# Turning the first groups' a and b with all 128 lanes, and one walk of 320 columns in the first batch's token mixing

## The chip, the cores and the metric

The kernel runs on one core of a Trainium2 chip (trn2). The metric is the device time of one execution in microseconds (us): the median of three runs. Engines are named as the profile does: PE is TensorE (PEld its weight loads), DVE is VectorE, ACT is ScalarE, POOL is GpSimd, SP is SyncE, which issues DMAs here.

## The reference

Three stages, all in float32 at the interface, with 4 batches, 8 heads, 768 steps, heads of 40, so rows of 320:

```python
# attention-like recurrence, per batch and head; state is 40 x 40
for t in range(S):
    y[t] = r[t] @ state
    Sa = state @ a[t]
    state = state * w[t][:, None] - outer(Sa, b[t]) + outer(v[t], k[t])
# x: the y of all heads, (4, 768, 320)
# first MLP block: mixing over the 768 steps (768 -> 256 -> 768), then over channels (320 -> 1536 -> 320)
u = x + (relu(x.T @ w_tok1) @ w_tok2).T
x = u + relu(u @ w_ch1) @ w_ch2
# second MLP block: normalised rows (320 -> 1280 -> 320)
x = x + relu(norm(x) * g_ln @ w2_ch1) @ w2_ch2
```

## The kernel before

The recurrence is done in chunks of 32 steps: within a chunk the state is not carried step by step, but a triangular system for the chunk is solved, and only from chunk to chunk is the state handed on (the chain). The 48 chain steps (function with L1069 and L1070) each treat half a pair of chunks for several heads; eight of them belong to one group G, and there are six groups. What is done for a group before its chain steps:

- `stack` (L781 to L802) loads w, b, a, k, v, r in 128 lanes of 32 steps, multiplies in the decays, splits each into high and low f16 parts in **one** buffer, o16 (L643, 128 lanes x 32 steps x 128), and stores it to scratch memory. The high parts are written by ACT (L795), the low part by DVE (L799) or POOL (L797). The next of the five can't be written before all readers of o16 are through.
- For groups 0 and 1, `turn` (L814 to L831) brings a and b from lanes x features to features x lanes on TensorE: o16 is the loaded operand, the identity the moving one. For later groups DMA transposes do this from scratch (`gram_load`, L833 to L840). The turned a stays for the chain ("at", eight single tiles, NA = 8); the turned b of groups 0 and 1 is put into the space of a weight matrix that is not needed yet ("d2").
- `gram` (L842 to L864) multiplies them into the 32 x 32 triangles, stores them (l_d); `solve` (L866 to L892) loads the triangles of the group ("ug"), sets diagonal and upper part with two selections on POOL (L870, L872), runs 30 pairs of DVE products and additions (L878, L880), and stores the result (t_d), from which the chain's operands are loaded ("tu").

Beside this run the decoding of the weights into f16 parts (L1153 load, L1158 and following on DVE, ACT) and, per batch, once its six pairs of chunks are through, the token mixing: `token_load` brings six row tiles "xt" of 128 x 320, `token1` multiplies them with w_tok1 into 256 hidden rows (two blocks NJ of 128) in two walks z over 160 columns each, with three-term f16 splits (L1245 on ACT, L1246 on DVE) and a relu (L1264, L1265); `token2` multiplies with w_tok2 (L1258) and adds (L1260). Then follow `feat_split` and the channel MLPs (L1307, L1310, L1317). Batch 0 uses the banks "pa", the others another one.

The order of the instructions on each engine is not that of the code: a planner (`Graph`, `fix_order`, L256 to L549) lists all instructions, gives each a duration from a table (`cost`, L201 to L235), schedules them by due times in several trials, takes the shortest, and writes the order of each engine as dependences without semaphores.

Of the kernel before, what the change touches and what calls it, by code (L numbers as in the profile page):

```python
# [20 lines left out]
def p2(n):  # L21
    return float(2.0 ** n)
# [178 lines left out]
def cost(i, engine):  # L201
# [23 lines left out]
        return 625 if len(rows) > 1 or 64 in rows or turned else 450, size / piece * (9 + piece / 27) / k * (1.6 if turned else 1.05)  # L225
    if engine == "PE":
        t = (free(i.outs[0]) + 6) / 2.4
        return (max(16, t / 2) if mode(i) else max(25, t)), 0
    part = 90 if min(x.ap[0][1] for x in aps) < 64 else 0
    if engine == "Activation":  # L230
# [322 lines left out]
def tile_main(  # L553
# [125 lines left out]
    PG = TG  # L679
    HC = C // 2  # L680
    RPP = PG * H * C
    NA = 8
    scr = {}
    l_d, t_d = {}, {}
    for G in range(NG // TG):
# [123 lines left out]
    def t_steps(G):  # L809
# [2 lines left out]
        st_i = {}  # L812

        def turn(n):  # L814
            for i in range(4):
                st = st_i.setdefault(i, {})
                if n == "a":
                    st[n] = stk.tile([128, TU * 128], F16, name="at", bufs=NA)
                    st_t.setdefault(4 * G + i, {})["a"] = st[n]
                else:  # L820
                    st[n] = wt["d2"].rearrange("p m l c -> p (m l c)")[:, i * TU * 128:(i + 1) * TU * 128]
                ls = slice(32 * i, 32 * i + 32)
                for t0 in (0, 16):
                    pt = ps_b.tile([128, 512], F32, name="pb", tag="b")[0:120].rearrange("p (l t) -> p l t", t=16)
                    for t in range(16):
                        nc.tensor.matmul(pt[:, :, t], o16[ls, t0 + t, 0:120], ident[ls, ls], start=True, stop=True)  # L826
                    dst = st[n][0:120].rearrange("p (l t) -> p l t", t=HC)[:, :, t0:t0 + 16]
                    if t0:
                        V.tensor_copy(dst, pt)
                    else:  # L830
                        A.activation(out=dst, in_=pt, func=ACTF.Copy)  # L831

        def gram_load(i):  # L833
            r0 = i * TU * 128
            st = st_i[i] = {}
            st["a"] = stk.tile([128, TU * 128], F16, name="at", bufs=NA)
            st["b"] = pre.tile([128, TU * 128], F16, name="tt_b", tag="st", bufs=2)
            for n in "ab":
                nc.sync.dma_start_transpose(out=st[n], in_=scr[n, G][r0:r0 + TU * 128, :])
            st_t.setdefault(4 * G + i, {})["a"] = st["a"]  # L840
# [68 lines left out]
    x_t = {}  # L909
# [326 lines left out]
    def token1(bb, z):  # L1236
        if z == 0:
            h16[bb] = moe.tile([128, NJ, 2, DM], F16, name="h16", bufs=1)
        n0 = DM // 2
        cs = slice(z * n0, (z + 1) * n0)  # L1240
        ps = token_bank(bb)[:, 0:NJ * n0].rearrange("p (j x) -> p j x", j=NJ)
        acc = Acc()
        for i in range(NT):
            x, o = x_t[bb][i][:, cs], moe.tile([128, 2, n0], F16, name="x16", bufs=2)
            nc.scalar.activation(out=o[:, 0, :], in_=x, func=ACTF.Copy, scale=p2(E_X))  # L1245
            nc.vector.scalar_tensor_tensor(out=o[:, 1, :], in0=x, scalar=p2(E_X),  # L1246
                                           in1=o[:, 0, :], op0=ALU.mult, op1=ALU.subtract)
            for jt in range(NJ):
                for n, (l, m) in enumerate(T3):
                    acc.mm(ps[:, jt, :], wt["t1"][:, i, l, jt * 128:(jt + 1) * 128], o[:, m, :], stop=i == NT - 1 and n == 2)  # L1250
        relu_split(ps, h16[bb][:, :, 0, cs], h16[bb][:, :, 1, cs])

    def token2(bb, i):
        x = x_t[bb][i]
# [22 lines left out]
    def feat_split(srcs, e, first=None):  # L1277
        ut = moe.tile([128, 6, TB * 128], F16, name="ut", bufs=2)
        for i, s in enumerate(srcs):
            u16 = moe.tile([128, 2, 384], F16, name="u16", bufs=2)  # L1280
            if first is not None:
                square("u", first + i, u16[:, 0, 0:64], s[:, 0:320:5])
            if first is None:
# [203 lines left out]
```

## Time and profile before

| | |
|---|---|
| median of three runs | 1177.3 us (1176.42 to 1181.52) |
| the profiled execution | 1180.47 us, span 1178.8 us, mean granted TensorE clock 0.979 |
| busy time in the span | PE 904.6, PEld 734.4, DVE 770.8, ACT 507.4, POOL 206.3 us |
| DMA | 161.67 MB in 356903 packets, 66.6% of the 16 engines' span on the hardware queue |

Busy time is summed over the whole span; its share hides that the stages have different limits, so the stages are shown apart in the rows below. A matmul's duration in a row runs from start to result; matmuls overlap, so that a group's duration divided by its count is the pace.

### The profile page before, as it was taken

To read this page: it belongs to the slowest core of one execution; us is meant where nothing else is said; L and a number is where in the kernel's file an instruction comes from. 1 tells how busy PE (TensorE), PEld (TensorE's weight loads), DVE (VectorE), ACT (ScalarE), POOL (GpSimd) and SP (SyncE) were. 2 spreads that over 40 slices of the span, in tenths; PEclk is the share of its full clock that TensorE was granted. 3 is DMA by queue.
4 is the path that set the end of the run, shared out by engine and by line. 5 is a ranking of instruction groups with operands and counts; after the bars stand their busy time and mean duration, and the time that the engine had idled before them with its cause. 6 is when DMAs were issued, how large, how long until landed. Compare 5 with 4: busy or idle time off the path is not lost.

```text
span 1178.8 us, 39814 instructions
## 1 busy us (share of the span) xinstructions
PE 904.6 (77%) x17422; PEld 734.4 (62%) x17422; DVE 770.8 (65%) x1936; ACT 507.4 (43%) x1105; POOL 206.3 (17%) x212
## 2 busy tenths in 40 slices
PE   0631450155588878899899999898999999999996
PEld 0620440154577756677677777676777888787774
DVE  6679485868977695657865689656964563443432
ACT  1443333455655453554445545554553343332221
POOL 0235450332000631034120052201000000000000
PEclk9999999999999989989999999999999999999998
DMA  5569826879998778958999757897565532221111
GB/s 159 155 171 242 189 72 193 260 146 182 229 190 162 179 157 198 186 102 160 154 204 162 166 118 170 144 174 173 111 115 93 80 47 47 52 44 21 36 17 26
DMA packets 356903, 161.67 MB, mean 137 GB/s; under 512 B 327536, under 2 KB 336752, under 8 KB 353136
## 3 DMA queue, kind: packets, MB, share of 16 engines
q1 hardware_dynamic: 356720, 159.04, 66.6%
q8 instruction: 138, 2.26, 0.8%
q14 instruction: 45, 0.37, 0.1%
HBM read 71.70 MB, written 50.59 MB: 104 GB/s over the span
## 4 chain that ended last, share of the span: by engine, by line
PE 34%; DVE 8%; DMA 4%; ACT 2%; issue 1%; SPq 1%; POOL 0%; DVEq 0%; ACTq 0%
PE pb L1317 12%; PE pa L1307 9%; PE ch L935 4%; PE pa L1310 3%; PE ps L935 3%; DVE ug L880 1%; DVE hh L1265 1%; PE ps L1014 1%; PE ps L1258 1%; DMA xt<-x_d 1%; DVE tmp L878 1%; DVE u L890 1%; PE ps L993 1%; DMA x<-in_v_dram 1%; DMA x<-in_r_dram 1%
## 5 line engine op out<-in xcount | busy, mean ns | idle before, releaser
L1317 PE MATMUL pb<-c,hh 128*128 128x320 f16 x864 | 179.5, 305 | 2.8 <-ACT hh L1264 2.1
L1317 PEld LDWEIGHTS <-hh 128*128 128x128 f16 x1584 | 153.4, 99 | 39.1 <-ACT hh L1264 3.0
L1265 DVE SCALAR_TENSOR_TENSOR hh<-pa,hh 128x512 f16<-128x512 f32 x132 | 90.6, 687 | 125.8 <-ACT hh L1264 125.3
L1307 PE MATMUL pa<-ut,c 128*128 128x256 f16 x864 | 159.4, 275 | 4.8 <-issue 2.4
L1264 ACT ACTIVATE hh<-pa 128x512 f16<-128x512 f32 x132 | 78.5, 595 | 173.0 <-PE pa L1310 168.2
L1317 PE MATMUL pb<-d,hh 128*128 128x320 f16 x720 | 147.6, 301 | 0.9 <-ACT hh L1264 0.7
L1307 PE MATMUL pa<-ut,d 128*128 128x256 f16 x720 | 137.7, 279 | 9.1 <-DVE hh L1265 6.2
L1307 PEld LDWEIGHTS <-c 128*128 128x128 f16 x864 | 83.4, 99 | 25.7 <-issue 5.3
L1307 PEld LDWEIGHTS <-d 128*128 128x128 f16 x720 | 69.8, 100 | 25.8 <-issue 8.2
L795 ACT ACTIVATE o<-x 128x2560 f16<-128x2560 f32 x30 | 69.9, 2331 | 20.9 <-DMA x<-in_a_dram 7.2
L880 DVE TENSOR_TENSOR ug<-ug,tmp 128x30 f32<-128x30 f32 (+9 forms) x180 | 73.0, 405 | 1.4
L878 DVE TENSOR_TENSOR tmp<-ug 128x30 f32<-128x30 f32 (+9 forms) x180 | 69.5, 386 | 4.2 <-POOL ug L872 2.6
L1343 POOL TENSOR_TENSOR y<-ve,mhalf 128x2 f32<-128x2 f32 x12 | 8.9, 741 | 353.3 <-DVE stats L1339 214.6
L826 PE MATMUL pb<-ident,o 32*120 32x32 f16 x512 | 50.3, 283 | 23.8 <-POOL o L797 13.2
L1310 PE MATMUL pa<-ut,c1t 128*128 128x256 f16 x288 | 65.4, 276 | 0.0
L826 PEld LDWEIGHTS <-o 32*120 32x120 f16 x512 | 49.1, 214 | 24.7 <-POOL o L797 13.4
L797 POOL TENSOR_TENSOR o<-x,o 128x1280 f16<-128x1280 f32 x15 | 49.7, 3314 | 59.2 <-ACT o L795 40.3
L935 PEld LDWEIGHTS <-srx 64*64 64x64 f16 x2304 | 51.8, 122 | 10.8 <-issue 8.1
L1310 PE MATMUL pa<-ut,d1t 128*128 128x256 f16 x240 | 55.5, 277 | 0.0
L858 PE MATMUL pa<-at,d 120*32 120x32 f16 (+1 forms) x384 | 5.2, 206 | 63.9 <-DVE lc L862 61.3
L935 PE MATMUL ch<-vx,sak 64*64 64x40 f16 x1152 | 33.9, 198 | 26.4 <-DVE n L1087 16.7
L722 POOL TENSOR_TENSOR x<-x,sx 128x1280 f32<-128x1280 f32 x10 | 33.1, 3307 | 115.7 <-DMA x<-in_k_dram 63.5
(204 smaller groups left out, 1914.2 us busy)
## 6 DMA issues: line engine op xcount, KB each, us to landing
raw<-in_moe_w_ch_dram SPq DMA_DIRECT2D x30, 320.0 KB
scr_b<-o SPq DMA_DIRECT2D x6, 1024.0 KB
scr_k<-o SPq DMA_DIRECT2D x6, 1024.0 KB
scr_v<-o SPq DMA_DIRECT2D x6, 1024.0 KB
scr_r<-o SPq DMA_DIRECT2D x6, 1024.0 KB
t_d<-u SPq DMA_DIRECT2D x24, 256.0 KB
tu<-t_d SPq DMA_DIRECT2D x24, 256.0 KB
scr_a<-o SPq DMA_DIRECT2D x4, 1024.0 KB
```

The costliest lines, as they stand in the source:

```text
L722: eng.tensor_tensor(out=o, in0=x, in1=y, op=ALU.mult)
L795: A.activation(out=hi2, in_=x.unsqueeze(2).broadcast_to([128, HC, 2, D]), func=ACTF.Copy, scale=p2(e))
L797: P.tensor_tensor(out=o16[:, :, lo:lo + D], in0=x, in1=o16[:, :, 0:D], op=ALU.subtract)
L826: nc.tensor.matmul(pt[:, :, t], o16[ls, t0 + t, 0:120], ident[ls, ls], start=True, stop=True)
L878: V.tensor_tensor(out=tv, in0=ug[:, 0:s, s:s + 1].broadcast_to([128, s, n]), in1=ug[:, s:s + 1, s + 1:32].broadcast_to([128, s, n]), op=AL ...
L880: V.tensor_tensor(out=ug[:, 0:s, s + 1:32], in0=ug[:, 0:s, s + 1:32], in1=tv, op=ALU.add)
L935: m = nc.tensor.matmul(out, lhsT, rhs, start=start, stop=stop, skip_group_check=True)
L1264: nc.scalar.activation(out=hi, in_=ps, func=ACTF.Relu)
L1265: nc.vector.scalar_tensor_tensor(out=lo, in0=ps, scalar=0.0, in1=hi, op0=ALU.max, op1=ALU.subtract)
L1307: nc.tensor.matmul(o, w1[:, f, l, ms], ut[:, f + 3 * q, :], start=n == 0, stop=False)
L1310: nc.tensor.matmul(o, w1t[:, ms], ut[:, 2 + 3 * q, :], start=False, stop=q == 1)
L1317: nc.tensor.matmul(pb[i][:, 0:DM], hh[:, l, c0:c0 + 128], w2[:, m0 + s, q, :], start=m0 + s == 0 and n == 0, stop=m0 + s == nm - 1 and n == 2)
```

## The change

Three edits in the kernel, and one in the planner's table. (1) `turn` for a group writes one tile of 4 x 1024 columns ("at", two buffers in all, which the DMA-transposed groups share), and each matmul takes all 128 lanes of o16 at once with the whole identity: 32 matmuls of 128 columns for a turn where there were 128 of 32 columns, with an output column in every fourth word of PSUM (every sixteenth before). Eight evictions of 120 x 512 as before, each now for four steps of all lanes. (2) the planner's table gives such a matmul with separated outputs at least 100. (3) `token1` for batch 0 walks the tiles once with 320 columns into two banks. The other batches are unchanged. (4) The splits of that walk share a tag with those of `feat_split`.

```diff
--- before.py
+++ after.py
@@ -225,6 +225,8 @@
         return 625 if len(rows) > 1 or 64 in rows or turned else 450, size / piece * (9 + piece / 27) / k * (1.6 if turned else 1.05)
     if engine == "PE":
         t = (free(i.outs[0]) + 6) / 2.4
+        if i.outs[0].ap[-1][0] > 1:
+            return max(100, t), 0
         return (max(16, t / 2) if mode(i) else max(25, t)), 0
     part = 90 if min(x.ap[0][1] for x in aps) < 64 else 0
     if engine == "Activation":
@@ -679,7 +681,7 @@
     PG = TG
     HC = C // 2
     RPP = PG * H * C
-    NA = 8
+    a_t = {}
     scr = {}
     l_d, t_d = {}, {}
     for G in range(NG // TG):
@@ -812,28 +814,30 @@
         st_i = {}
 
         def turn(n):
+            if n == "a":
+                o = a_t[G] = stk.tile([128, 4, TU * 128], F16, name="at", bufs=2)
+            else:
+                o = wt["d2"].rearrange("p m l c -> p (m l c)")[:, 0:4 * TU * 128].rearrange("p (i c) -> p i c", i=4)
             for i in range(4):
-                st = st_i.setdefault(i, {})
+                st_i.setdefault(i, {})[n] = o[:, i]
                 if n == "a":
-                    st[n] = stk.tile([128, TU * 128], F16, name="at", bufs=NA)
-                    st_t.setdefault(4 * G + i, {})["a"] = st[n]
+                    st_t.setdefault(4 * G + i, {})["a"] = o[:, i]
+            dst = o[0:120].rearrange("p i (l t) -> p (i l) t", t=HC)
+            for t0 in range(0, HC, 4):
+                pt = ps_b.tile([128, 512], F32, name="pb", tag="b")[0:120].rearrange("p (l t) -> p l t", t=4)
+                for t in range(4):
+                    nc.tensor.matmul(pt[:, :, t], o16[:, t0 + t, 0:120], ident, start=True, stop=True)
+                if t0 % 8:
+                    V.tensor_copy(dst[:, :, t0:t0 + 4], pt)
                 else:
-                    st[n] = wt["d2"].rearrange("p m l c -> p (m l c)")[:, i * TU * 128:(i + 1) * TU * 128]
-                ls = slice(32 * i, 32 * i + 32)
-                for t0 in (0, 16):
-                    pt = ps_b.tile([128, 512], F32, name="pb", tag="b")[0:120].rearrange("p (l t) -> p l t", t=16)
-                    for t in range(16):
-                        nc.tensor.matmul(pt[:, :, t], o16[ls, t0 + t, 0:120], ident[ls, ls], start=True, stop=True)
-                    dst = st[n][0:120].rearrange("p (l t) -> p l t", t=HC)[:, :, t0:t0 + 16]
-                    if t0:
-                        V.tensor_copy(dst, pt)
-                    else:
-                        A.activation(out=dst, in_=pt, func=ACTF.Copy)
+                    A.activation(out=dst[:, :, t0:t0 + 4], in_=pt, func=ACTF.Copy)
 
         def gram_load(i):
             r0 = i * TU * 128
             st = st_i[i] = {}
-            st["a"] = stk.tile([128, TU * 128], F16, name="at", bufs=NA)
+            if i == 0:
+                a_t[G] = stk.tile([128, 4, TU * 128], F16, name="at", bufs=2)
+            st["a"] = a_t[G][:, i]
             st["b"] = pre.tile([128, TU * 128], F16, name="tt_b", tag="st", bufs=2)
             for n in "ab":
                 nc.sync.dma_start_transpose(out=st[n], in_=scr[n, G][r0:r0 + TU * 128, :])
@@ -1236,6 +1240,10 @@
     def token1(bb, z):
         if z == 0:
             h16[bb] = moe.tile([128, NJ, 2, DM], F16, name="h16", bufs=1)
+        if bb == 0:
+            if z == 0:
+                wide(bb)
+            return
         n0 = DM // 2
         cs = slice(z * n0, (z + 1) * n0)
         ps = token_bank(bb)[:, 0:NJ * n0].rearrange("p (j x) -> p j x", j=NJ)
@@ -1250,6 +1258,20 @@
                     acc.mm(ps[:, jt, :], wt["t1"][:, i, l, jt * 128:(jt + 1) * 128], o[:, m, :], stop=i == NT - 1 and n == 2)
         relu_split(ps, h16[bb][:, :, 0, cs], h16[bb][:, :, 1, cs])
 
+    def wide(bb):
+        ps = [token_bank(bb) for _ in range(NJ)]
+        for i in range(NT):
+            x, o = x_t[bb][i], moe.tile([128, 2, DM], F16, name="x16", tag="u16", bufs=2)
+            nc.scalar.activation(out=o[:, 0, :], in_=x, func=ACTF.Copy, scale=p2(E_X))
+            nc.vector.scalar_tensor_tensor(out=o[:, 1, :], in0=x, scalar=p2(E_X),
+                                           in1=o[:, 0, :], op0=ALU.mult, op1=ALU.subtract)
+            for jt in range(NJ):
+                for n, (l, m) in enumerate(T3):
+                    nc.tensor.matmul(ps[jt][:, 0:DM], wt["t1"][:, i, l, jt * 128:(jt + 1) * 128], o[:, m, :],
+                                     start=i == 0 and n == 0, stop=i == NT - 1 and n == 2)
+        for jt in range(NJ):
+            relu_split(ps[jt][:, 0:DM], h16[bb][:, jt, 0], h16[bb][:, jt, 1])
+
     def token2(bb, i):
         x = x_t[bb][i]
         pu = token_bank(bb)
@@ -1277,7 +1299,7 @@
     def feat_split(srcs, e, first=None):
         ut = moe.tile([128, 6, TB * 128], F16, name="ut", bufs=2)
         for i, s in enumerate(srcs):
-            u16 = moe.tile([128, 2, 384], F16, name="u16", bufs=2)
+            u16 = moe.tile([128, 2, 384], F16, name="u16", tag="u16", bufs=2)
             if first is not None:
                 square("u", first + i, u16[:, 0, 0:64], s[:, 0:320:5])
             if first is None:
```

The planner moves other instructions as a result. On POOL, between the suffix and inverse work of group 1's decays (L722, L724 after; the two lines more in the code shift all later numbers), the order before had the two selections of group 0's solve ("ug") ahead of the low parts of b and a (o) of group 1:

```order
L722 TENSOR_TENSOR wf<-wf 128x7x40
L722 TENSOR_TENSOR x<-x,sx 128x1280
L722 TENSOR_TENSOR wf<-wf 128x40
L870 AFFINE_SELECT ug<-ug 128x1024
L722 TENSOR_TENSOR wf<-wf 128x40
L872 AFFINE_SELECT ug<-ug 128x1024
L797 TENSOR_TENSOR o_118<-x,o_118 128x32x40
L722 TENSOR_TENSOR wf<-wf 128x40 x5
L722 TENSOR_TENSOR wf<-wf 128x8x120
L722 TENSOR_TENSOR x<-x,wf 128x1280
L797 TENSOR_TENSOR o_118<-x,o_118 128x32x40
```

and the order after has the low parts of b (the first o) and of a (the second) ahead of the selections:

```order
L724 TENSOR_TENSOR wf<-wf 128x7x40
L799 TENSOR_TENSOR o_118<-x,o_118 128x32x40
L724 TENSOR_TENSOR wf<-wf 128x40 x7
L724 TENSOR_TENSOR wf<-wf 128x8x120
L724 TENSOR_TENSOR x<-x,wf 128x1280
L799 TENSOR_TENSOR o_118<-x,o_118 128x32x40
L874 AFFINE_SELECT ug<-ug 128x1024
L876 AFFINE_SELECT ug<-ug 128x1024
L724 TENSOR_TENSOR x<-x,sx 128x1280
L799 TENSOR_TENSOR o_118<-x,o_118 128x32x40
```

The two selections moved behind two writes of o16 and the work between them. On SP, the load of "ug" of group 0 stood ahead of the store of r of group 0 (scr_r_123) and the store of b of group 1 (scr_b_129):

```order
L868 DMA ug<-l_d_125 128x1024
L714 DMA scr_r_123<-o_118 128x4096
L711 DMA x<-in_a_dram 32x1x1280 x2
L954 DMA_TRANSPOSE kt<-scr_k_120 128x1024
L1153 DMA raw<-in_moe_w_ch_dram 64x768 x4
L1153 DMA raw<-in_moe_w_ch_dram 128x640
L954 DMA_TRANSPOSE rt<-scr_r_123 128x1024
L711 DMA x<-in_a_dram 32x1x1280 x2
L711 DMA x<-in_k_dram 32x1x1280
L714 DMA scr_b_129<-o_118 128x4096
```

and now stands behind both, and behind the fourth store of the triangles (l_d):

```order
L716 DMA scr_r_123<-o_118 128x4096
L713 DMA x<-in_a_dram 32x1x1280 x2
L1157 DMA raw<-in_moe_w_ch_dram 64x768 x4
L868 DMA l_d_125<-sab 128x8x32
L1157 DMA raw<-in_moe_w_ch_dram 128x640
L958 DMA_TRANSPOSE kt<-scr_k_120 128x1024
L958 DMA_TRANSPOSE rt<-scr_r_123 128x1024
L713 DMA x<-in_a_dram 32x1x1280 x2
L713 DMA x<-in_k_dram 32x1x1280
L716 DMA scr_b_129<-o_118 128x4096
L713 DMA x<-in_k_dram 32x1x1280
L872 DMA ug<-l_d_125 128x1024
```

The load moved behind both stores. On DVE, the token mixing of batch 0 before: L1246 are the low parts of the second walk's tiles, between the pairs of a solve and the chain, L1265 a walk's relu, L1260 the first addition of the second matrix:

```order
L1246 SCALAR_TENSOR_TENSOR x_12691<-xt,x_12691 128x160
L880 TENSOR_TENSOR ug<-ug,tmp 128x12x19
L980 TENSOR_TENSOR srx<-ps,srx 128x512
L878 TENSOR_TENSOR tmp<-ug 128x234
L1265 SCALAR_TENSOR_TENSOR h_7189<-pa,h_7189 128x2x160
L880 TENSOR_TENSOR ug<-ug,tmp 128x13x18
L878 TENSOR_TENSOR tmp<-ug 128x238
L880 TENSOR_TENSOR ug<-ug,tmp 128x14x17
L878 TENSOR_TENSOR tmp<-ug 128x240
L880 TENSOR_TENSOR ug<-ug,tmp 128x15x16
L1260 SCALAR_TENSOR_TENSOR xt<-pa,xt 128x320
```

and after, where L1266 is the last tile's low part of the single walk, L1287 its two relus and L1282 the addition:

```order
L1266 SCALAR_TENSOR_TENSOR x_6844<-xt,x_6844 128x320
L1142 SCALAR_TENSOR_TENSOR yo<-ps,yw 128x320
L1074 SCALAR_TENSOR_TENSOR r_6593<-ch,r_6593 128x160
L882 TENSOR_TENSOR tmp<-ug 128x30
L884 TENSOR_TENSOR ug<-ug,tmp 128x30
L1287 SCALAR_TENSOR_TENSOR h_6796<-pa,h_6796 128x320 x2
L882 TENSOR_TENSOR tmp<-ug 128x58
L1080 SCALAR_TENSOR_TENSOR sas<-ch,sas 128x4x40
L884 TENSOR_TENSOR ug<-ug,tmp 128x2x29
L1282 SCALAR_TENSOR_TENSOR xt<-pa,xt 128x320
```

The additions stand ahead of the solve's pairs that were before them, and fewer rows lie between a relu and the first addition. The later walks of the other batches are as they were.

## Rows read from the trace of the kernel before

**Rows 1.** Stages: us, busy us (instructions) of PE, PEld, DVE, ACT, POOL; clock; DMA; GB/s.

```profile
0.00:121.00 121.00, 32.84 (x548) 31.19 (x548) 86.48 (x187) 42.54 (x76) 40.34 (x68) 1.00 0.73 181
121.00:199.00 78.00, 27.95 (x384) 27.16 (x385) 48.53 (x121) 25.23 (x40) 27.68 (x11) 1.00 0.51 140
199.00:246.00 47.00, 10.17 (x420) 9.06 (x420) 37.92 (x84) 26.63 (x55) 16.59 (x6) 1.00 0.78 222
246.00:427.00 181.00, 134.51 (x3539) 115.28 (x3539) 146.30 (x362) 96.92 (x227) 34.68 (x37) 1.00 0.97 188
427.00:1012.00 585.00, 545.30 (x11111) 427.62 (x11110) 388.30 (x1013) 276.64 (x625) 84.92 (x87) 0.96 0.73 135
1012.00:1178.00 166.00, 153.79 (x1422) 124.07 (x1421) 63.30 (x174) 39.38 (x85) 2.07 (x3) 0.98 0.17 31
```

**Rows 2.** Timeline, DVE: chain steps 2, 16 and 32 of 48.

```profile
245.74 0.30 DVE L1070 SCALAR_TENSOR_TENSOR r<-ch,r 128x160 f16<-128x160 f32 x1
...
427.08 0.32 DVE L1070 SCALAR_TENSOR_TENSOR r<-ch,r 128x160 f16<-128x160 f32 x1
...
730.66 0.33 DVE L1070 SCALAR_TENSOR_TENSOR r<-ch,r 128x160 f16<-128x160 f32 x1
```

**Rows 3.** Timeline, group 0: start us, us, instruction [idle before <-releaser].

```profile
48.13 2.34 ACT L795 ACTIVATE o<-x 128x2560 f16<-128x2560 f32 x1 [1.00 <-PE pb L826]
...
52.88 11.89 PE L826 MATMUL pb<-ident,o 32*120 32x32 f16 x128 [4.79 <-DVE o L799]
...
64.87 2.34 ACT L795 ACTIVATE o<-x 128x2560 f16<-128x2560 f32 x1 [1.06 <-PE pb L826]
```

**Rows 4.** A turn's evictions, tile pb (count: min/median/max ns, first to last).

```profile
L829 DVE CAST d<-pb x8: 691/692/692, 37.5 to 140.8; 120x512 f16<-120x512 f32 x8
```

**Rows 5.** Matmuls near the new one: tile pb, timeline, page's group (mean ns).

```profile
L1100 PE MATMUL pb<-ident,sas x48: 314/314/363, 233.0 to 376.9; 128*120 128x128 f16 x48
...
397.72 0.63 PE L1100 MATMUL ps<-ident,sas 128*120 128x128 f16 x4
...
L1317 PEld LDWEIGHTS <-hh 128*128 128x128 f16 x1584 | 153.4, 99 | 39.1 <-ACT hh L1264 3.0
```

**Rows 6.** Timeline, turns of group 1.

```profile
131.69 9.06 PE L826 MATMUL pb<-ident,o 32*120 32x32 f16 x96
...
150.08 6.23 PE L826 MATMUL pb<-ident,o 32*120 32x32 f16 x64 [9.33 <-POOL o L797]
```

**Rows 7.** Timeline, DVE: first product and last addition of the solve, a wait between.

```profile
120.99 0.19 DVE L878 TENSOR_TENSOR tmp<-ug 128x30 f32<-128x30 f32 x1 [2.63 <-POOL ug L872]
...
189.71 0.33 DVE L1158 TENSOR_SCALAR wst<-raw 128x320 int32<-128x320 int32 x1 [13.75 <-DMA raw<-in_moe_w_ch_dram]
...
198.27 0.20 DVE L880 TENSOR_TENSOR ug<-ug,tmp 128x30 f32<-128x30 f32 x1
```

**Rows 8.** Timeline, token mixing of batch 0 on ACT, PE and DVE.

```profile
409.89 0.42 ACT L1264 ACTIVATE h<-pa 128x320 f16<-128x320 f32 x1
421.19 0.44 ACT L1264 ACTIVATE h<-pa 128x320 f16<-128x320 f32 x1
...
418.12 1.76 PE L935 MATMUL pa<-x,t 128*128 128x160 f16 x12 [1.97 <-DVE x L1246]
...
424.92 0.49 DVE L1260 SCALAR_TENSOR_TENSOR xt<-pa,xt 128x320 f32<-128x320 f32 x1
...
425.62 1.68 PE L1258 MATMUL pa<-h,t 128*128 128x320 f16 x6
427.19 0.84 PE L1258 MATMUL pa<-h,t 128*128 128x320 f16 x5
...
440.21 1.06 PE L1307 MATMUL pa<-ut,c 128*128 128x256 f16 x6
```

**Rows 9.** Issues of SyncE for the tile at, and for the solves' tile ug.

```profile
L839 SPq DMA_TRANSPOSE at<-scr_a x16: 1173/1709/4062, 254.8 to 734.5; - x16
...
L868 SPq DMA_DIRECT2D ug<-l_d x6: 529/608/1790, 112.0 to 797.3; - x6
```

## Prediction

> **What bounds the kernel now.** I read first the table of stages [rows 1]. The reader is to see six stages with different limits. From 427 us on TensorE (PE) is busy 545.30 of 585.00 us and then 153.79 of 166.00: what remains there as idle time is 39.7 + 12.2 = 51.9 us, so after 427 the end is set by the amount of TensorE work. Before 427 it isn't: TensorE works 32.84 of 121, 27.95 of 78, 10.17 of 47 and 134.51 of 181 us. Time is to be had or lost there, and 427 us is where the channel MLPs, which can fill TensorE, begin (first matmul of L1307 at 440.21 [rows 8]). What holds the early stages is, in turn: the preparation of the first two groups, in which b, a, k, v, r pass one after the other through the one buffer o16 (0 to 121); the triangular solve of group 0 (121 to 199); the way from it to the chain (199 to 246: the second chain step is at 245.74 [rows 2]); and then DMA, busy 0.97, with VectorE (DVE) at 146.30 of 181.00 us (246 to 427).
>
> The chain's steps [rows 2] are the clock of the middle: DVE instructions of L1070, the second at 245.74, the sixteenth at 427.08. Then come the rows of the turns [rows 3 to 6], of the solve [rows 7], of the token mixing of batch 0 [rows 8] and of the loads of later groups [rows 9].
>
> **Edit 1, the turns of a and b of groups 0 and 1.** Before, one turn is 128 matmuls with 32 rows and 32 columns each. It takes 11.89 us where it runs alone [rows 3] (93 ns apiece); 64 of them take 6.23 and 96 take 9.06 [rows 6]. Meanwhile o16 can't be overwritten: the next scaling by ACT (L795) starts at 48.13 and at 64.87, and the profile names the turn as what released it [rows 3]. After, a turn has 32 matmuls with 128 columns, and eight evictions as before, of the same size. The nearest row to the new matmul is L1100: four matmuls with identity, 128x128, in 0.63 us [rows 5]; one of them lasts 0.314 at the longest usual [rows 5], so the pace is (0.63 − 0.31) / 3 = 0.107 us and 32 make 3.4 us. But two "pb" banks alternate, and each bank has to be evicted before its next filling: 4 × 0.107 + 0.2 to the last result + 0.69 for the VectorE eviction [rows 4] + about 0.3 of hand-over = 1.6 us for a bank, so eight fillings over two banks take 4 × 1.6 = 6.4 us. The 0.2 is 0.314 less the pace; the 0.3 is an estimate, two releases from engine to engine at 0.10 (the turn ends at 52.88 + 11.89 = 64.77, ACT starts at 64.87 [rows 3]) and as much again. I take 6.4, which gains 11.9 − 6.4 = 5.5 us a turn. Ends: a gain of 6.5 if the hand-over is free, and none at all if the output, written now every 16 bytes, is slow. No row shows a 128-column matmul into separated words; the row that bounds it is the old turn, whose outputs lie 64 bytes apart: 32 columns in 93 ns are at most 93 / 32 = 2.9 ns a column, or 0.37 us for 128 columns, 11.9 us a turn, the old time. I go by the low end of the price, since the old pace has another explanation in the same rows: each matmul also loads 120 weight columns, and the loads of L1317, 128 columns and no separated words, average 99 ns [rows 5].
>
> The Trainium skill, "PSUM — Partial Sum Buffer", section "Specifications (TRN2)", says that PSUM lines are 8 bytes long and that any non-contiguous pattern slows matmuls significantly. By it each column would pay, and the turn would stay near 11.9 us. "TensorE: Matmul & The Clock Gate", section "LDWEIGHTS", has a load take about its columns over 1.2 in ns, which is 100 ns for 120 columns, and leaves nothing of the old pace for the separated words; the 93 ns agree with it. No run here tells which holds for 128 columns; the first is the third rival below.
>
> The buffer's chain is b0, a0, ..., b1, a1. The turn of b0 gains about 1 (ACT waited 1.00 on PE there [rows 3]); a0 and b1 gain 5.5 each. So o16 of a1, ready when its turn starts at 150.08 [rows 6], is ready 12 us earlier, at 138; the turn of a1 gives 5.5 more to what follows.
>
> **Edit 2, the order around the solve.** With the turns shorter, GpSimd (POOL) gets the two selections of the solve of group 0 after the low part of a1 instead of before that of b1, and SyncE the load of the solve's tile ("ug") after the store of b1. Before, the solve's first DVE product is at 120.99, right after the second selection [rows 7]. After, the selections stand behind a1's write: 138 + 2.7 = 141, some 20 us later. The solve before ran from 120.99 to its last addition at 198.27 [rows 7], 77.3 us, in which VectorE was busy 48.53 of 78.00 [rows 1]: 29.5 us were idle time, 13.75 of them in one piece on a weight load that stands in DVE's queue ahead of the solve's rest [rows 7]. Started at 141 it ends at 141 + 48 = 189 if every wait is over by then, and at 218 if none is. I take the middle, 204: about 6 us late (bounds −9 and +20). Queued behind it are the t_d stores on SyncE and the first chain steps, so this shift is passed on to the step at 245.74.
>
> **Edit 3, what VectorE has to do between chain steps 2 and 16.** In the new order 321 DVE instructions stand between the second and the sixteenth L1070, where 362 stood. 41 × 146.30 / 362 = 41 × 0.404 = 16.6 us of work are gone from a stretch in which DVE is busy 0.81. Most of it is weight decoding (11 instead of 16 groups) and solving (34 pairs instead of 45) that now lie in the earlier trough, so it costs nothing there: DVE has 29.5 us idle in 121 to 199. But DMA is busy 0.97 of the same stretch and its bytes do not change. Late next, if DVE isn't, is DMA. I count half: −8 us (bounds 0 and −16.6).
>
> **Edit 4, token mixing of batch 0.** Before, the six row tiles are walked twice with 160 columns. The first walk's relu is at 409.89, the second's at 421.19 [rows 8], and the second mixing matrix follows. Now one walk with 320 columns ends where the first ended, plus a second relu: 36 matmuls with 320 columns instead of 72 with 160, about the same time on TensorE (12 of the old take 1.76 us, 0.15 each or 10.6 for 72; six 320-column matmuls take 1.68 in the same stretch [rows 8], 10.1 for 36), and six ACT and six DVE instructions less, worth 2 or 3 us beside other work. It starts the second matrix and with it the MLP at 440.21 about 10 us earlier against its tiles (bounds 0 and −11.3). The clock matters for the size: just there six matmuls of L1258 take 1.68 us and the next five 0.84 [rows 8], 0.28 and 0.17 apiece: times of the lower (1.2 GHz) and of the upper level (2.4), though the granted clock of the stage reads 1.00 throughout [rows 1]. What comes earlier runs part of the way at the lower level. The tiles of the walk share a two-deep ring with the feature splits; that is covered, as the splits come after the mixing.
>
> **Edit 5, one "at" tile with two buffers instead of eight singles.** A load for group G waits until all four pairs of group G−2 are through with theirs. Group 5 is the tightest: group 3 ends with chain step 32, at 730.66 [rows 2]; before, the last single was loaded at 734.5, and the load of its solve is issued at 797.3 [rows 9]. All four loads can follow 730.66 and their products still come before 797.3. I cost it at nothing; the cover is those 60 us.
>
> **Sum.** +6 (solve) − 8 (VectorE) − 10 (mixing) = −12 us at the point where TensorE fills. What comes earlier lands in a stage where TensorE was already busy 134.51 of 181.00 us, and 51.9 us of idle remain behind it that depend on other waits; I let about 0.8 pass: −10. The profiled execution took 1180.47 us (span 1178.8, 1.7 around it), 3.2 above the median of 1177.3. 1177.3 − 10 = **1167 us**.
>
> **Rivals.**
> First (the forecast, 0.50): as summed, own range 1156 to 1176.
>
> Second, nothing arrives (0.20): the solve keeps its waits and its 77 us (+20), and this uses up −8 and −10: 1177, between 1172 and 1182. For it: the waits inside the solve name DMA, which is no faster. Against: DMA's share is 0.51 in 121 to 199, so loads there can come earlier.
>
> Third, slower (0.15): the separated words make a new matmul take 0.37 us. Then the turn stays at 11.9, a1 is written at 150 and the solve, behind it in the new order, starts at 152.7, 31.7 late; with its 77 us and −8, −10 that is +13.7 at 427, × 0.8 = +11: 1188. It decides from where the turn takes more than the 6.4 us of the sum; at 8 us the loss is some +4. For it speaks that no row shows this output; against it the weight loads.
>
> Fourth, all gains pass (0.10): the solve ends at 189 (−9), DVE gives 16.6 and mixing 11.3: −37 × 0.8 = −30: 1148.
>
> Fifth (0.05): the two-deep ring of "at" stops SyncE's queue, in which loads for everything else stand, behind a pair's last use; a stop of one pair, two chain steps of (427.08 − 245.74) / 14 = 13 us [rows 2], against the 12 of the sum gives +14 × 0.8 = +11, 1188. Against it stand the 60 us above.
>
> **How the numbers follow.** A measurement of this kernel can't tell less than 0.5%, 5.9 us, from no change. Faster than 1171.4: four fifths of the first (0.40), all of the fourth (0.10), a little of the second (0.03): 0.53. Slower than 1183.2: 0.13 of the third, 0.04 of the fifth, 0.03 of the second: 0.20. The rest, 0.27, is no change. The range leaves out most of the fourth and half of the third: 1151 to 1187.
>
> **What would show it.** Right if a turn of group 0 takes 5 to 8 us, the second selection of the first solve ends at 138 to 145, the solve ends by 210, and the second chain step is at 240 to 256; if the sixteenth step is no later than 425; if the first second-matrix addition (L1260 before, at 424.92 [rows 8]) is at 408 to 418; and if TensorE's idle time from there to the end is still about 52 us. The step on edit 1 is wrong if the turns take 10 us or more; that on edit 2 if the solve ends after 215 or before 190; that on edit 3 if DMA takes up the room and the steps from 2 to 16 stay 181 us apart; the last factor if the MLP begins 10 us earlier and the end does not move.

## The result, and the profile after

The changed kernel takes 1158.0 us in the median (1155.46 to 1161.89, four runs) beside 1176.9 of the kernel before on the same chip: a ratio of 0.985, 95% interval 0.981 to 0.989. The forecast was 1167, its range 1151 to 1187. The profiled execution took 1157.96 us, its span 1156.3, where it was 1178.8. Line numbers from here on are those of the changed kernel, unless another run is named: `turn` is L829 (matmul), L831 and L833 (evictions), a chain step L1074, the mixing L1270 (first matrix), L1286 (relu), L1280 and L1282 (second matrix and its addition), the MLP begins with L1329.

The same stages as in [rows 1], the last one ending with the span (us; busy us and instructions of PE, PEld, DVE, ACT, POOL; granted clock; DMA share; GB/s):

```profile
0.00:121.00 121.00, 29.68 (x404) 24.95 (x404) 89.25 (x198) 48.84 (x85) 47.80 (x74) 0.68 0.82 207
121.00:199.00 78.00, 9.21 (x192) 8.37 (x193) 64.28 (x155) 31.36 (x54) 22.89 (x8) 0.52 0.63 177
199.00:246.00 47.00, 14.15 (x508) 12.37 (x509) 33.83 (x72) 24.90 (x52) 19.38 (x14) 0.50 0.80 203
246.00:427.00 181.00, 143.12 (x3695) 118.55 (x3692) 134.59 (x349) 96.69 (x226) 26.26 (x28) 0.59 0.92 173
427.00:1012.00 585.00, 544.88 (x11105) 434.93 (x11103) 384.82 (x1008) 273.35 (x614) 82.11 (x86) 0.95 0.71 133
1012.00:1156.00 144.00, 132.91 (x1111) 106.65 (x1108) 54.49 (x151) 32.09 (x70) 2.07 (x3) 0.98 0.15 28
```

The reader is to see the trough of 121 to 199: VectorE is busy 64.28 us instead of 48.53, DMA 0.63 instead of 0.51. That is work brought forward, and 427 to 1012 is as full as before (544.88 against 545.30); the time is missing at the end, 144 us instead of 166. The clock column is not to be compared in the early stages: it reads about 0.5 to 0.7 here and 1.00 before, yet the same matmul of L1104 (L1100 before) on "pb" has a median of 314 ns in both. The trace's clock records begin at 34.26 us here and only at 427.07 in the kernel before; ahead of its first record the column reads 1.00.

The chain and the mixing, from the timeline of DVE, ACT and PE (start, duration), for [rows 2, 8]:

```profile
238.68 0.32 DVE L1074 SCALAR_TENSOR_TENSOR r<-ch,r 128x160 f16<-128x160 f32 x1
...
406.81 0.31 DVE L1074 SCALAR_TENSOR_TENSOR r<-ch,r 128x160 f16<-128x160 f32 x1
...
392.97 0.44 ACT L1286 ACTIVATE h<-pa 128x320 f16<-128x320 f32 x1 [0.36 <-PE pa L1270]
...
395.87 0.49 DVE L1282 SCALAR_TENSOR_TENSOR xt<-pa,xt 128x320 f32<-128x320 f32 x1 [0.92 <-PE pa L1280]
...
413.51 1.49 PE L1329 MATMUL pa<-ut,c 128*128 128x256 f16 x6
```

Step 2 is 7.1 us earlier than before, step 16 20.3, the first addition of the second matrix 29.1 (it was at 424.92), the MLP 26.7, the end of the span 22.5.

The four turns and what stands behind them, from the timeline of the same kernel, for [rows 3, 6, 7]:

```profile
28.95 4.61 PE L829 MATMUL pb<-ident,o 128*120 128x128 f16 x20 [6.34 <-DVE o L801]
...
35.74 0.60 PE L829 MATMUL pb<-ident,o 128*120 128x128 f16 x4 [0.69 <-ACT d L833]
...
40.29 3.75 PE L829 MATMUL pb<-ident,o 128*120 128x128 f16 x16 [2.62 <-DVE o L801]
...
47.17 0.60 PE L829 MATMUL pb<-ident,o 128*120 128x128 f16 x4 [0.50 <-DVE at L831]
...
108.55 2.82 PE L829 MATMUL pb<-ident,o 128*120 128x128 f16 x12 [5.03 <-POOL o L799]
114.53 1.87 PE L829 MATMUL pb<-ident,o 128*120 128x128 f16 x8 [3.16 <-DVE d L831]
...
119.30 1.11 PE L829 MATMUL pb<-ident,o 128*120 128x128 f16 x4
...
130.70 6.25 PE L829 MATMUL pb<-ident,o 128*120 128x128 f16 x28 [10.29 <-POOL o L799]
...
132.19 1.28 POOL L876 TENSOR_SCALAR_AFFINE_SELECT ug<-ug 128x1024 f32<-128x1024 f32 x1
...
186.87 0.20 DVE L884 TENSOR_TENSOR ug<-ug,tmp 128x30 f32<-128x30 f32 x1
```

The turn of a in group 0 lasts from 40.29 to 47.77, 7.5 us instead of 11.9. The turn of b in group 1 runs from 108.55 to 120.41 on TensorE, 11.9 us, as long as the old one of a in group 0; 3.16 us of it are one wait for an eviction by VectorE. Four matmuls take 0.60 us in some places and 1.11 in others. The turn of a in group 1 lasts from 130.70 to 140.30, 9.6 us. The selections end at 133.47, the solve at 187.07.

The turn of b in group 0 is the one that gained most, and [rows 3] do not show its length before. There, too, 128 matmuls, from the timeline of the kernel before:

```profile
34.06 6.23 PE L826 MATMUL pb<-ident,o 32*120 32x32 f16 x64 [5.23 <-DVE o L799]
...
40.87 3.31 PE L826 MATMUL pb<-ident,o 32*120 32x32 f16 x32 [0.58 <-DVE d L829]
...
44.69 3.40 PE L826 MATMUL pb<-ident,o 32*120 32x32 f16 x32
```

It held o16 from 34.06 to 48.09, 14.0 us; now it is 28.95 to 36.34, 7.4.

### The profile page after: what moved, and what is told of

It reads as the page before. It is cut to its first block, busy times and chain, and to the rows that moved or that the text cites. A ratio compares the mean times of both kernels' runs of the same rounds, so it can differ in the third digit from the quotient of the medians.

```text
span 1156.3 us, 38954 instructions
## 1 busy us (share of the span) xinstructions
PE 873.9 (76%) x17002; PEld 705.8 (61%) x17002; DVE 761.3 (66%) x1930; ACT 507.2 (44%) x1099; POOL 200.5 (17%) x212
## 5 line engine op out<-in xcount | busy, mean ns | idle before, releaser
L1339 PE MATMUL pb<-c,hh 128*128 128x320 f16 x864 | 172.2, 301 | 0.0
L1287 DVE SCALAR_TENSOR_TENSOR hh<-pa,hh 128x512 f16<-128x512 f32 x132 | 90.7, 688 | 121.2 <-ACT hh L1286 120.8
L1329 PE MATMUL pa<-ut,c 128*128 128x256 f16 x864 | 155.6, 278 | 4.3 <-DVE hh L1287 4.3
L1286 ACT ACTIVATE hh<-pa 128x512 f16<-128x512 f32 x132 | 78.4, 594 | 157.8 <-PE pa L1332 146.4
L1339 PE MATMUL pb<-d,hh 128*128 128x320 f16 x720 | 141.0, 299 | 0.5 <-DVE xt L1349 0.5
L1329 PE MATMUL pa<-ut,d 128*128 128x256 f16 x720 | 133.9, 278 | 4.5 <-DVE hh L1287 4.1
L1329 PEld LDWEIGHTS <-c 128*128 128x128 f16 x864 | 84.1, 100 | 24.5 <-issue 4.6
L1329 PEld LDWEIGHTS <-d 128*128 128x128 f16 x720 | 70.4, 100 | 22.2 <-issue 4.4
L882 DVE TENSOR_TENSOR tmp<-ug 128x30 f32<-128x30 f32 (+9 forms) x180 | 73.5, 408 | 3.1 <-DMA kb<-scr_b 1.1
L884 DVE TENSOR_TENSOR ug<-ug,tmp 128x30 f32<-128x30 f32 (+9 forms) x180 | 69.1, 384 | 1.8
L981 DVE TENSOR_TENSOR ps<-ps,causal 128x512 f32<-128x512 f32 x60 | 41.6, 694 | 23.1 <-PE ps L997 22.7
L724 POOL TENSOR_TENSOR sx<-sx 128x40 f32<-128x40 f32 (+2 forms) x50 | 22.6, 461 | 184.9 <-DVE sx L750 183.0
L939 PEld LDWEIGHTS <-kb 64*40 64x40 f16 x2112 | 41.5, 102 | 18.5 <-issue 17.1
L829 PE MATMUL pb<-ident,o 128*120 128x128 f16 x128 | 27.3, 443 | 32.6 <-POOL o L799 15.3
L799 POOL TENSOR_TENSOR o<-x,o 128x1280 f16<-128x1280 f32 x15 | 44.0, 2934 | 42.9 <-ACT o L797 28.2
```

The source lines that it names most:

```text
L799: P.tensor_tensor(out=o16[:, :, lo:lo + D], in0=x, in1=o16[:, :, 0:D], op=ALU.subtract)
L829: nc.tensor.matmul(pt[:, :, t], o16[:, t0 + t, 0:120], ident, start=True, stop=True)
L882: V.tensor_tensor(out=tv, in0=ug[:, 0:s, s:s + 1].broadcast_to([128, s, n]), in1=ug[:, s:s + 1, s + 1:32].broadcast_to([128, s, n]), op=AL ...
L884: V.tensor_tensor(out=ug[:, 0:s, s + 1:32], in0=ug[:, 0:s, s + 1:32], in1=tv, op=ALU.add)
L939: m = nc.tensor.matmul(out, lhsT, rhs, start=start, stop=stop, skip_group_check=True)
L981: V.tensor_tensor(out=sm, in0=sm, in1=causal.unsqueeze(1).broadcast_to([128, 8, 64]), op=ALU.mult)
```

## The experiments

Theory T, as first put, was that the start (turns) and the mixing gain separately, and that what they gain adds up. Its rivals were that only the mixing matters (M), that the separated words still hold back the start (S), and that the order which the planner happens to give counts as much as the edits (L). Later two more stand against L: that the two edits gain only together (I), and that the turns alone gain nothing but for one lucky order (I2). Each is written in the expectation of the run that it speaks of.

**turn_only**: the changed kernel without the single walk.

```diff
     def token1(bb, z):
         if z == 0:
             h16[bb] = moe.tile([128, NJ, 2, DM], F16, name="h16", bufs=1)
-        if bb == 0:
-            if z == 0:
-                wide(bb)
-            return
```

> The new turns and the shared at tile, with the token mixing of batch 0 in two walks of 160 columns as before; the order is planned anew. Theory T (two gains that add: the chain starts and runs 14 us earlier by the time batch 0's rows are there, the mixing itself is 15 us shorter, and about 0.78 of what is gained there reaches the end): the turns' share alone, 14 x 0.78 = 11 us, 1166 us; second chain step near 239, first second-matrix addition near 411. Rival M (only the mixing matters, what the start gains is lost on the way): 1175 to 1179. Rival L (the planner's order is what changed, by luck, and any other plan would be as far off): no relation to the edit, anywhere from 1158 to 1185, and the milestones of the start don't move together with the end.

Measured 1178.4 us, ratio 1.0005 (0.998 to 1.003): no gain. T's 1166 is missed; M's number is met, and L's wide range too. But its start is nearly as early as that of the changed kernel (step 2 at 241.57, sixteenth at 411.22, 3 and 4 us later), so the loss came later.

**mix_only**: the kernel before with these lines, `wide` (cut here; it is that of the change) and the shared tag.

```diff
+        if bb == 0:
+            if z == 0:
+                wide(bb)
+            return
```

> The kernel before with only the single walk of 320 columns for batch 0's token mixing; turns as before, order planned anew. T: from chain step 12 to the first second-matrix addition some 30 us instead of 44.7, and the end 15 x 0.78 = 12 us earlier, 1165 us. M: all of the gain, 1158 to 1160. L: no relation.

Measured 1172.6, ratio 0.9965 (0.9935 to 0.9995). Neither T nor M: the parts alone gain nothing (turns) and 4 us (mixing), both together 19. From step 12 to the first addition it took 39.1 us instead of 51.1 (51.1, not the 44.7 that the expectation says, is 424.92 less step 12 at 373.82).

**contig**: the changed kernel with the same order and adjacent words in PSUM. TURNS names these matmuls to the planner's table, which goes on pricing them at 100 or more, so that the order stays.

```diff
-pt = ps_b.tile(...)[0:120].rearrange("p (l t) -> p l t", t=4)
+pt = ps_b.tile(...)[0:120].rearrange("p (t l) -> p t l", t=4)
-nc.tensor.matmul(pt[:, :, t], o16[:, t0 + t, 0:120], ident, start=True, stop=True)
+m = nc.tensor.matmul(pt[:, t], o16[:, t0 + t, 0:120], ident, start=True, stop=True)
+TURNS.add(m.ins.name)
-V.tensor_copy(dst[:, :, t0:t0 + 4], pt)
+V.tensor_copy(dst[:, :, t0:t0 + 4], pt.rearrange("p t l -> p l t"))
...
```

> The changed kernel in the very same order on every engine, but each turn's matmul writes 128 adjacent words of PSUM, and the evictions read them in the old sequence, each 512 bytes from the last. If the separated words slow the matmul, four of them take 0.63 us at the lower clock instead of 1.11 and 0.45 or less instead of 0.60 at the upper; if it is the weight load, 1.11 and 0.60 stay. The evictions stay at 0.60 and 0.69 us if the distance of the words doesn't matter for ACT and DVE, more otherwise. T: the turns of group 1 end 1 to 4 us earlier, and the end moves by 0 to 3 us (1155 to 1158). Rival S (the separated words still hold back the start): 5 us or more, 1153 or less.

Measured 1156.2, ratio 0.9812 (0.977 to 0.986); beside the 0.985 of the changed kernel the difference is not resolved. S's 1153 is not reached, but 5 us are within the two intervals, so S is not excluded at the end. At the milestones of the profiled executions the separated words do hold back the start: the turns of group 1 end at 115.29 and 135.97 (120.41 and 140.30 in the changed kernel), step 2 is at 234.43 and the first addition at 389.93, 4.3 and 5.9 us earlier in the same order. In a second order (contig_t3 beside other_plan, below) they came 1.7 and 3.2 us later, so what the start gains is not settled. The price of the separated words is. Tile "pb" of the changed kernel (count: min/median/max ns, first and last start), then of contig, in contig's own line numbers, with lines of its timeline:

```profile
L829 PE MATMUL pb<-ident,o x128: 269/502/502, 28.9 to 139.9; 128*120 128x128 f16 x128
...
L833 ACT ACTIVATE d<-pb x8: 597/598/598, 30.1 to 119.1; 120x512 f16<-120x512 f32 x8
L831 DVE CAST d<-pb x8: 676/684/692, 30.9 to 120.4; 120x512 f16<-120x512 f32 x8
```

```profile
L830 PE MATMUL pb<-ident,o x128: 264/314/363, 28.5 to 135.7; 128*120 128x128 f16 x128
...
L1106 PE MATMUL pb<-ident,sas x48: 219/314/363, 223.8 to 353.4; 128*120 128x128 f16 x48
...
L835 ACT ACTIVATE d<-pb x8: 580/598/599, 29.2 to 114.4; 120x512 f16<-120x512 f32 x8
L833 DVE CAST d<-pb x8: 677/686/692, 29.6 to 115.3; 120x512 f16<-120x512 f32 x8
...
105.34 1.11 PE L830 MATMUL pb<-ident,o 128*120 128x128 f16 x8 [5.02 <-POOL o L800]
...
111.23 1.01 PE L830 MATMUL pb<-ident,o 128*120 128x128 f16 x8 [3.94 <-DVE d L833]
...
113.64 0.68 PE L830 MATMUL pb<-ident,o 128*120 128x128 f16 x4
```

Adjacent words: 314 ns for one, 0.58 to 0.68 us for four. That this is the lower level is taken from L1106, also 128 adjacent columns, which has the same 314 ns as its median on "pb" there (219 at the least). Separated: 502 ns and 1.11 us where the granted clock of the changed kernel is 0.50 (the lower level, 108 to 121 us), 0.60 for four where it is 1.00 (the upper, 44.5 to 48). For the pace the longer groups are the better rows, as the first matmul of a group often differs from the rest: twelve separated ones take 2.82 us at 108.55, (2.82 − 0.50) / 11 = 0.21 us; eight adjacent ones take 1.01 to 1.11, so (1.01 − 0.31) / 7 = 0.10 to 0.11. Inside the groups the starts in the two traces lie 0.213 and 0.107 us apart: twice. The evictions don't notice whether their words lie 4 or 512 bytes apart: 598 and 684 ns against 598 and 686.

**other_plan**: the changed kernel in another of the planner's orders.

```diff
-ROUNDS = 10
+ROUNDS = 6
```

> The changed kernel, instruction for instruction, but the planner stops after 6 trials instead of 10 and takes another order. T: the order is worth little beside the edits, 1154 to 1164. L: the order is worth as much as the edits, 1168 or more, or 1148 or less.

Measured 1154.7, ratio 0.9814 (0.977 to 0.986), within T. In this order the solve of group 0 stands early (its last addition starts at 170.01) and step 2 is at 218.12, 20 us ahead of the changed kernel's; in the medians hardly anything is left of them at the end.

So the parts do not add, and one other order, of one set of instructions, could not decide on L. The next runs take single edits and the kernel before in other orders: that of the planner's trial k (the last one that it makes), whether or not its own estimate is the shortest.

```diff
-        best = min(best, trial, key=lambda t: t[0])
+        best = trial
-ROUNDS = 10
+ROUNDS = 7
```

**before_t3alt** (the kernel before, trial 7):

> The kernel before, instruction for instruction, in another order: that of the planner's seventh trial instead of the one it chose. Theory I (turns and mixing gain only together, the order itself is worth little): 1172 to 1182. Rival L (each set of instructions has a spread of 10 us and more over the planner's orders, and single sums of the edits can't be read from one order each): outside of that.

1174.0, ratio 0.9965 (0.993 to 1.000): within I.

**turn_t3** (turns alone, trial 3):

> The new turns alone with the old mixing, in the order of the planner's third trial. I: again no gain, 1173 to 1183. L: this set of instructions in its own order was an unlucky draw; here 1160 to 1170, which is what the sum of separate gains gives (1166).

1160.1, ratio 0.983 (0.978 to 0.988): what L said. These are the same instructions as in turn_only, 18 us apart in two orders.

**mix_t3** (single walk alone, trial 3):

> The single walk alone with the old turns, in the order of the planner's third trial. I: 1168 to 1177, as in its own order (1172.6). L: 1160 to 1167, or above 1178.

1189.6, ratio 1.009 (1.006 to 1.013): L again, 17 us above its own order. A comparison of one order with one can't price an edit here.

**contig_t3** (both edits, adjacent words, the order of other_plan):

> Both edits with adjacent words in PSUM, in the order that the kernel other_plan has (third trial). Two gains of the earlier runs put together, 1.8 us from the adjacent words and 3.3 from the order: 1153, range 1148 to 1157, under I and L alike; the turns at the lower clock at 0.63 us for four matmuls.

1154.2, ratio 0.980 (0.975 to 0.986): the lowest ratio, but not resolved from other_plan or contig, nor from the changed kernel.

**before_t4, turn_t8, mix_t5, after_t9**: a third order of each of the four sets.

> The kernel before in a third order (fourth trial). Theory L: the two edits shift the middle of a set's times, and each order lies up to 10 us to either side. From the orders run so far the middles are 1176 without an edit, so 1170 to 1184 here; second chain step at 244 to 250, 47 to 52 us from chain step 12 to the first second-matrix addition. Rival I2 (the turns alone bring nothing but for one lucky order): says nothing else here.

1174.0, ratio 0.997 (0.993 to 1.001): within L; step 2, at 254.34, is above its bound of 250.

> The new turns with the old mixing in a third order (eighth trial). L: the middle is the sum's 1166, so 1160 to 1173; second chain step before 243 and sixteenth before 412 as in both other orders, whatever the end. I2: 1174 to 1182.

1170.4, ratio 0.996 (0.991 to 1.000): within L in the end; its step 2 is at 248.83 and step 16 at 415.79, later than expected.

> The single walk with the old turns in a third order (fifth trial). L: between the two others (1172.6 and 1189.6), 1166 to 1184; second chain step at 244 to 250 as in all kernels with the old turns; 37 to 45 us from chain step 12 to the first second-matrix addition. I2: no gain, above 1174.

1177.7, ratio 1.002 (0.998 to 1.005): within L's 1166 to 1184, and no gain, as I2 says too. Step 2 at 254.19 lies above the bound.

> The changed kernel in a third order (ninth trial). L: 1150 to 1164; second chain step before 243, 37 to 42 us from step 12 to the first second-matrix addition. Against L and for the two edits gaining nothing by themselves: above 1168.

1168.7, ratio 0.994 (0.990 to 0.997): a miss for L, 4.7 above its range and 0.7 above the bound that speaks for edits without a gain of their own. Step 2 is as expected (237.87), and from step 12 to the first addition it takes 35.5 us instead of 37 to 42.

All together, three orders of each set, without the two runs with adjacent words (median of all executions; from the one profiled execution of each the start of chain steps 2, 12 and 16, of the first addition of the second matrix, and the span's end, which can lie some 10 us from the median):

| set, order | median | step 2 | step 12 | step 16 | first addition | end |
|---|---|---|---|---|---|---|
| before, own | 1177.3 | 245.7 | 373.8 | 427.1 | 424.9 | 1178.8 |
| before, 7 | 1174.0 | 247.9 | 366.7 | 416.7 | 417.3 | 1166.2 |
| before, 4 | 1174.0 | 254.3 | 374.2 | 427.6 | 424.6 | 1175.9 |
| mixing, own | 1172.6 | 248.9 | 372.8 | 418.5 | 411.9 | 1169.5 |
| mixing, 3 | 1189.6 | 246.2 | 374.0 | 424.3 | 418.6 | 1198.2 |
| mixing, 5 | 1177.7 | 254.2 | 379.9 | 428.9 | 420.2 | 1181.4 |
| turns, own | 1178.4 | 241.6 | 362.6 | 411.2 | 406.9 | 1179.6 |
| turns, 3 | 1160.1 | 216.3 | 344.3 | 388.0 | 393.6 | 1163.9 |
| turns, 8 | 1170.4 | 248.8 | 366.6 | 415.8 | 414.0 | 1174.6 |
| both, own | 1158.0 | 238.7 | 356.5 | 406.8 | 395.9 | 1156.3 |
| both, other_plan | 1154.7 | 218.1 | 347.6 | 387.4 | 384.5 | 1144.3 |
| both, 9 | 1168.7 | 237.9 | 354.6 | 408.3 | 390.2 | 1169.4 |

The means of the medians are 1175.1, 1180.0, 1169.6 and 1160.5. The changed instructions are 14.6 us ahead of those before, with three orders that span 14 us; the turns are worth 5.5 us without the single walk and 19.5 with it, 12.5 on the mean; the single walk −5 and +9, 2 on the mean. With up to 18 us between orders of one set, a gain of the turns at the end is likely and the walk's share there is open.

At the milestones it is clearer. The turn of a in group 1, for which o16 must be ready, starts at 132.6 to 150.1 us in the six orders with the old turns (mean 142.6) and at 126.7 to 130.7 with the new (129.3): 13 us apart, and the ranges do not meet. Step 12 is at 373.6 on the mean with the old turns (366.7 to 379.9) and at 355.3 with the new (344.3 to 366.6): the two ranges only touch. From step 12 to the first addition it takes 48.9 us in two walks (44.4 to 51.1) and 39.3 in one (35.5 to 44.6).

What is gained at the first addition is then partly given back. From there to the end the kernel before takes 754, 749 and 751 us, the nine others 758 to 780. Each of these is one execution. The row for that stretch, of the kernel before, the changed one and mix_t3 (columns as in [rows 1]):

```profile
424.90:1178.80 753.90, 701.19 (x12564) 553.17 (x12564) 453.61 (x1191) 317.09 (x713) 86.99 (x90) 0.97 0.61 112
```

```profile
395.90:1156.30 760.40, 703.38 (x12644) 561.45 (x12642) 465.73 (x1222) 321.77 (x719) 92.11 (x92) 0.95 0.62 115
```

```profile
418.60:1198.20 779.60, 715.69 (x12592) 568.12 (x12590) 461.96 (x1208) 320.38 (x717) 88.78 (x91) 0.93 0.58 111
```

About the same number of matmuls, but the granted clock goes 0.97, 0.95, 0.93, and with it TensorE's busy time 701, 703, 716 and its idle time 53, 57, 64. In the changed kernel the longest piece at the lower level after 427 us (from 611 to 642) lies in these rows:

```profile
560.00:580.00 20.00, 19.54 (x273) 15.14 (x271) 17.84 (x45) 12.86 (x25) 5.62 (x3) 1.00 1.11 178
580.00:600.00 20.00, 16.41 (x219) 12.94 (x220) 7.13 (x14) 6.36 (x10) 0.00 (x0) 0.83 0.81 142
600.00:620.00 20.00, 15.13 (x391) 12.04 (x390) 9.73 (x25) 5.68 (x15) 5.29 (x8) 0.78 1.10 201
620.00:640.00 20.00, 14.84 (x463) 13.26 (x463) 10.32 (x24) 11.95 (x29) 0.00 (x0) 0.50 1.03 146
```

TensorE falls from 19.54 to 14.84 of 20 us busy and the clock to the lower level. The kernel before, in the last of these stretches:

```profile
620.00:640.00 20.00, 17.75 (x516) 13.74 (x506) 9.25 (x23) 10.19 (x26) 0.00 (x0) 0.96 1.01 146
```

The reading that suggests itself is that work done earlier is missing there, where TensorE then waits for the chain. Between 540 and 720 us the longest unbroken piece at the lower level is 7 to 14 us in the three orders of the kernel before, 27 to 34 in those of the changed one and 41 in mix_t3. But it is not all of the loss: turn_only, with 773 us from the first addition to the end, has none above 10.2 us there. No run filled the hole alone, so neither its cause nor its price is shown.

## Why the prediction was right, and where not

The direction and the outline held: the gain is made before TensorE fills, arrives there as an earlier first addition, and passes for the most part (22.5 of 29.1 us, 0.77; 0.8 was taken). But the forecast's 10 us were half of the 19, and of the three terms of its sum one stood as put. Four of its own signs of being right failed on the early side: the second selection ends at 133.47 (138 to 145 was said), the solve at 187.07 (its step was to be wrong if before 190), step 2 is at 238.68 (240 to 256) and the first addition at 395.87 (408 to 418). That the time still fell into the range is in part luck, as the next points show.

- Mixing, −10: right. It is 9.6 us shorter from step 12 on over all orders. In this pair of kernels it is 39.4 instead of 51.1, so 11.7.
- The solve, +6: wrong in sign, step 2 came 7.1 earlier. The solve's start was forecast at 141 and is at 135.10; it took 52 us instead of the 63 of the sum, as VectorE idled 7.0 us inside it (45.00 of 51.97 busy) instead of 29.5. What the sum missed lies ahead of it: o16 of a1 was ready at 130.70, not 138. That placing the solve behind a1 costs time by itself agrees with the table: in turn_t3 and other_plan, where the solve starts ahead of the turn of a1 (at 112.47 and 91.44), step 2 is at 216 and 218, with the same turns in the other four kernels at 238 to 249.
- The way to a1, 12 us: 19.4 in this pair. The largest mis-sized term is the turn of b0, put at "about 1" from the 1.00 that ACT waited right before its write. That wait is only the last piece: the turn held o16 for 14.0 us and now holds it for 7.4, so it gained 6.6. With a start 5.1 us earlier, 4.4 from the turn of a0 and 0.8 between the two, a0's ends at 47.77 instead of 64.77. The start of b1, at 108.55 instead of 128.0, is another 2.4 ahead; from there to a1 nothing more is gained (the turn of b1 takes 11.9 us where it took 12.8, the wait behind it 10.3 where it was 9.3). Some of this is the draw of the order: over all orders the turn of a1 starts 13 us earlier, close to the 12 of the forecast, and in this pair 19.4.
- VectorE between steps 2 and 16, −8: the time came (181.3 to 168.1 us), but most of it is not the edits'. The kernel before takes 168.8 and 173.3 in its two other orders, mix_only and turn_only 169.7. Its own order was the slowest of the twelve, and counting 41 instructions fewer in an order read one draw as the effect of a change. Over all orders it is 174.3 us on the mean with the old turns (168.8 to 181.3) and 169.4 with the new (167.0 to 171.8); 5 us may be the turns', but the ranges overlap.
- The price of a turn, 6.4 us: on TensorE it is 7.4 (b) and 7.5 (a) in group 0, 11.9 and 9.6 in group 1, all above the 6.4. The step that failed is the choice of the low end for the matmul into separated words, 0.107 us: that is what adjacent words cost at the lower clock, as in the row L1100 it came from; separated ones cost 0.213. With 0.213 the same sum is 4 × (0.85 + 0.29 + 0.69 + 0.3) = 8.5 us. That the old pace, 32 columns in 93 ns, could come from the weight loads said nothing of 128 columns. The rule of the Trainium skill ("PSUM — Partial Sum Buffer", "Specifications (TRN2)") that a non-contiguous pattern slows matmuls was the better guide: the runs show 0.213 against 0.107 us in the same order.
- The third rival went by 0.37 us for a matmul, and the runs show 0.213. The turn of b in group 1 took its 11.9 us all the same, 3.16 of them in the wait for VectorE; in contig, with adjacent words, it took 9.9. Still the rival did not come: the solve starts 14 us later than before, not 31.7, since a1 was ready early for the reasons above, and removing the separated words moved the end by less than can be told.
- The ring of "at", at nothing: the loads run from 313.6 to 731.5 and the last solve's load is at 786.5, ahead of the 734.5 and 797.3 before.

What the prediction lacked is a term for the order itself. It read one order of each kernel as if the edits had made all of its differences; the runs put 3 to 18 us between orders of the same instructions.

## What to carry to other kernels

Where a planner sets the order, time each variant in several of its orders before pricing an edit: here the turns alone came out between no gain and 17 us by the order alone. Price an edit at the milestone next to it (here the start of a1's turn, step 12, and from there to the first addition), where the kernels with and without the edit part more clearly, and not at the end. Price the time for which a shared buffer is held, not the last wait in front of its next writer. Here a 128-column matmul into words 16 bytes apart cost twice an adjacent one, and moving the distance to the eviction's reads was free.

## What was not expected of the hardware

- An eviction of 120 x 512 reads words 512 bytes apart in PSUM as fast as adjacent ones (598 and 686 ns against 598 and 684), while the matmul that writes words 16 bytes apart pays double (0.213 us for 128 columns at the lower clock, 0.107 adjacent).
- The profile's clock column can stay at 1.00 for hundreds of us in one kernel and read 0.5 in the other, with the same durations of the same matmuls (314 ns): ahead of the first clock record of a trace (427.07 us in the kernel before, 34.26 in the changed one), durations tell the level better.
